# Expert stage of an attention-MoE kernel: nested blocks without else arms, one half block per expert behind the nest, and its branch announced in every block

## The chip, the cores and the metric

The kernel runs on one core of a Trainium2 chip. The metric is the device time of one execution in microseconds. A core has five engines with an instruction queue each: TensorE (PE), VectorE (DVE), ScalarE (ACT), GpSimd (POOL) and SyncE (SP). In the rows of the profile PE is shown as PE (matmuls) and PEld (weight loads); a name with q at its end (PEldq, ACTq, SPq) is what the sequencer of that engine does itself: jumps, register steps, semaphore steps.

## The reference

The work is attention inside chunks of 64 positions, a dense feed-forward layer, and a mixture of eight experts of which each token takes one:

```
attn = softmax over each chunk of 64 (q k^T / 8);  x = attn v, as 4608 tokens x 512
x    = relu(x @ w_in)^2 @ w_out                     # 512 -> 2048 -> 512
xn, en    = x and expert_emb, each row divided by its norm
expert    = argmax(xn @ en.T / tau);  gate = softmax(...)[expert]
for e in range(8):                                  # 512 -> 1024 -> 512
    out[tokens of e] = gate * (relu(x[tokens of e] @ w1[e]) @ w2[e])
```

How many tokens an expert has is known only on the chip. With the inputs of these runs experts 0 to 7 have 473, 448, 2029, 378, 256, 704, 192 and 128 tokens.

## The kernel before

The attention, the dense layer and the routing take the first 971 us and stand in straight code; the change touches of them only eight small operations behind the routing's last step (L499). The expert stage follows. Tokens of one expert are gathered from DRAM by their row numbers, 256 at a time (`TG`), turned by PE transposes (`turn`, L571), multiplied in three passes of a high and a low half with w1 (`first_product`, L594), passed through ReLU by ACT (L597) and DVE (L598), multiplied with w2 (`m2`, L413), scaled by the gate on ACT (L608) and scattered to the output by POOL (L609). Results of PE go through four PSUM banks in turn. 256 tokens are a full block; of the matmuls a full block has 96 of the first product, two second products of 24 and, between these, 8 transposes for the block that comes next. `short` (L960) is a half block of 128 tokens, with x as the stationary operand: 24 and 8 transposes (`sh`, `sht`) and 24, and with their weight loads some 116 instructions of PE.

The first block of an expert is straight code (`group`, L1020); in it, the weights of the next expert are loaded and split as well. For what is left, `more(e, g, ...)` (L990) is an `If` on the count: if more than 256 g + 128 tokens are there, a full block is computed and `more(e, g + 1)` stands inside it, 17 levels deep. Its else arm holds a second `If` (more than 256 g tokens?) around a half block. So the half block stands 17 times per expert in the program: first come the 17 full blocks in a row, then their else arms from the deepest one outwards, each ending with a semaphore step and a jump over the arms that follow. The way out of a nest at depth g is, on every engine: a jump to the else arm, taken because the count is too small; the second compare, which jumps over the half block or falls into it; a semaphore step that waits until what is queued on the engine is done; and, for g above 1, a jump over the other g - 1 arms to the next expert.

A jump can be announced: `mark_branch_hint_location` puts a register step and a hint instruction into each engine's queue that name the jump's place and whether it will be taken. Before, `more_e_(g+1)` is announced at the start of block g, and the jumps in and behind the else arm are not announced. Nothing reorders instructions around these places: each engine runs its queue in the order of the code, and PE's sequencer hands matmuls to a queue ahead of their execution, so that jumps are taken while earlier matmuls are still at work.

By the counts, experts 0 and 1 run two full blocks, expert 2 eight, expert 3 one and a half block, expert 4 one, expert 5 three, expert 6 one, and expert 7 only a half block. Expert 0's first block has run before 971 us.

## Time and profile before

| | us |
|---|---|
| median of three runs | 1430.68 (1430.56 to 1431.48) |
| the profiled execution, its own time | 1430.2 |
| its span in the profile | 1428.4 |
| PE busy in the span | 1367.7 (96%) |
| expert stage, from PE's first wait for its gathers to the end of the span | 971 to 1428.4 |

The busy share alone doesn't say where time could go: PE is close to full on average, and what idle time it has lies in few places. The view that lists PE's waits names what ended them; the timeline of PE gives their place; the instructions of the sequencer, grouped by line, give the length of each jump. A jump that the sequencer takes 4 us for is idle time of PE only as far as PE's queue runs empty behind it.

### The profile page before, as it was taken

To read this page: it belongs to the slowest core of one execution; us is meant where nothing else is said; L and a number is where in the kernel's file an instruction comes from. 1 tells how busy PE (TensorE), PEld (TensorE's weight loads), DVE (VectorE), ACT (ScalarE), POOL (GpSimd) and SP (SyncE) were. 2 spreads that over 40 slices of the span, in tenths; PEclk is the share of its full clock that TensorE was granted. 3 is DMA by queue.
4 is the path that set the end of the run, shared out by engine and by line. 5 is a ranking of instruction groups with operands and counts; after the bars stand their busy time and mean duration, and the time that the engine had idled before them with its cause. 6 is when DMAs were issued, how large, how long until landed. Compare 5 with 4: busy or idle time off the path is not lost. (4 is left out here: it accounts for less than half of the span.)

```text
span 1428.4 us, 27983 instructions
## 1 busy us (share of the span) xinstructions
PE 1367.7 (96%) x10780; PEld 1221.6 (86%) x10780; DVE 791.1 (55%) x2146; ACT 644.3 (45%) x1529; POOL 175.2 (12%) x189
## 2 busy tenths in 40 slices
PE   5699999999999999999999999998999999899998
PEld 4697889988998898899889988987889898788886
DVE  6878566657656675666576556754442222145424
ACT  4693535634553554355345535633442222145424
POOL 0000010000000100000100001323212121113110
PEclk6899999999999999999999999999999999999999
DMA  8533332122122212212212222136533111156412
GB/s 212 158 119 119 104 70 57 37 38 61 39 45 38 53 39 45 45 40 44 50 35 54 43 38 90 46 119 200 181 126 99 34 60 35 43 165 199 150 49 92
DMA packets 222794, 116.81 MB, mean 82 GB/s; under 512 B 191585, under 2 KB 192227, under 8 KB 222468
## 3 DMA queue, kind: packets, MB, share of 16 engines
q1 hardware_dynamic: 213508, 89.01, 23.9%
q0 software_dynamic: 9056, 25.35, 5.6%
q8 instruction: 99, 1.62, 0.5%
q14 instruction: 99, 0.81, 0.2%
q10 hardware_dynamic: 32, 0.02, 0.0%
HBM read 94.64 MB, written 20.19 MB: 80 GB/s over the span
## 5 line engine op out<-in xcount | busy, mean ns | idle before, releaser
L389 PE MATMUL l<-xT,wa 128*128 128x256 f32 x3168 | 382.6, 281 | 6.0 <-DVE wa L157 6.0
L389 PEld LDWEIGHTS l<-xT,wa 128*128 128x128 f32 x3168 | 378.1, 189 | 8.3 <-DVE wa L157 6.7
L413 PE MATMUL l<-wb,g 128*128 128x512 f32 x1536 | 373.2, 398 | 0.0
L413 PEld LDWEIGHTS l<-wb,g 128*128 128x128 f32 x1536 | 284.0, 188 | 65.7
L440 DVE CUSTOM_DVE_ANT_0 junk<-X,en 128x512 bf16<-128x512 f32 x240 | 166.3, 693 | 64.0 <-ACT X L433 60.8
L408 DVE TENSOR_TENSOR g<-l,g 128x256 fp32r<-128x256 f32 x264 | 110.3, 419 | 160.4 <-ACT g L405 157.1
L598 DVE SCALAR_TENSOR_TENSOR h<-m,h 128x256 fp32r<-128x256 f32 x144 | 60.9, 423 | 195.6 <-ACT h L597 189.0
L413 PE MATMUL m<-wa,h 128*128 128x512 f32 x576 | 139.3, 397 | 0.0
L399 ACT ACTIVATE l<-l 128x256 f32<-128x256 f32 x272 | 100.8, 371 | 68.6 <-PE l L389 60.7
L413 PEld LDWEIGHTS m<-wa,h 128*128 128x128 f32 x576 | 106.4, 188 | 24.2
L597 ACT ACTIVATE h<-m 128x256 fp32r<-128x256 f32 x144 | 55.1, 383 | 132.8 <-PE m L594 118.0
L405 ACT ACTIVATE g<-l 128x256 fp32r<-128x256 f32 x264 | 101.5, 384 | 8.5
L402 ACT ACTIVATE l<-l 128x256 f32<-128x256 f32 x272 | 100.1, 368 | 8.7
L490 POOL DMA_INDIRECT perm<-tid,pos x36 | 38.2, 1060 | 523.2 <-DVE pos L489 281.3
L594 PEld LDWEIGHTS m<-xc,wa 128*128 128x128 f32 x768 | 92.5, 189 | 0.6
L594 PE MATMUL m<-xc,wa 128*128 128x256 f32 x768 | 92.8, 281 | 0.0
L413 PE MATMUL m<-wb,h 128*128 128x512 f32 x336 | 81.9, 398 | 0.0
L609 POOL DMA_INDIRECT out_dram<-o,idx x38 | 38.5, 1014 | 326.9 <-ACT xc L79 140.1
L413 PEld LDWEIGHTS m<-wb,h 128*128 128x128 f32 x336 | 62.0, 188 | 14.1
L608 ACT ACTIVATE o<-m,gn 128x512 f32<-128x512 f32 x23 | 15.8, 688 | 114.6 <-PE m L413 71.2
L435 POOL TENSOR_TENSOR ss<-ss,half 128x1 f32<-128x1 f32 x36 | 28.1, 780 | 308.7 <-ACT l L434 165.2
L80 DVE TENSOR_TENSOR xc<-tp,xc 128x512 fp32r<-128x512 f32 x36 | 24.3, 684 | 69.1 <-ACT xc L79 69.1
(182 smaller groups left out, 1540.2 us busy)
## 6 DMA issues: line engine op xcount, KB each, us to landing
we<-in_moe_w_dram SPq DMA_DIRECT2D x124, 256.0 KB
v<-in_v_dram SPq DMA_DIRECT2D x144, 64.0 KB
x2d<-X SPq DMA_DIRECT2D x32, 258.0 KB
ws<-in_moe_w_in_dram SPq DMA_DIRECT2D x8, 1024.0 KB
ws<-in_moe_w_out_dram SPq DMA_DIRECT2D x8, 1024.0 KB
q<-in_q_dram SPq DMA_DIRECT2D x160, 32.0 KB
k<-in_k_dram SPq DMA_DIRECT2D x160, 32.0 KB
en<-embn SPq DMA_DIRECT2D x1, 2048.0 KB
```

The source lines that it names most:

```text
L389: PE.matmul(out=ps, lhsT=wi[:, a, m // 4, kt, (m % 4) * 128:(m % 4 + 1) * 128], rhs=x[b][:, :, kt, :], start=(n == 0), stop=(n == 3 * KD - 1),
L399: S.activation(out=ps, in_=ps, func=AF.Relu)
L402: S.activation(out=ps, in_=ps, func=AF.Square)
L405: S.activation(out=g[:, 0], in_=ps, func=AF.Copy)
L408: V.tensor_tensor(out=g[:, 1], in0=ps, in1=f32(g[:, 0]), op=ALU.subtract)
L413: PE.matmul(out=ps, lhsT=gs[kk][:, b, tt * 128:(tt + 1) * 128], rhs=wt[:, a, kk, :], start=(kk == 0 and n == 0), stop=(kk == last - 1 and ...
L440: V.tensor_tensor_reduce(out=junk.rearrange("p (g c) -> p g c", g=4), in0=rows(X)[:, :, 0:128], in1=en[:, e].rearrange("p (g c) -> p g c", ...
L490: G.indirect_dma_start(out=perm[:, :], out_offset=bass.IndirectOffsetOnAxis(ap=pos[:, 0:1], axis=0), in_=tid[:, i:i + 1], in_offset=None,)
L594: PE.matmul(out=ps, lhsT=v1[:, a, m // 4, kt, (m % 4) * 128:(m % 4 + 1) * 128], rhs=xt[:, b, :, kt, :], start=(n == 0), stop=(n == 3 * KD ...
L597: S.activation(out=g[:, 0], in_=ps, func=AF.Relu)
L598: V.scalar_tensor_tensor(out=g[:, 1], in0=ps, scalar=0.0, in1=f32(g[:, 0]), op0=ALU.max, op1=ALU.subtract)
L609: G.indirect_dma_start(out=out[:, :], out_offset=bass.IndirectOffsetOnAxis(ap=col, axis=0), in_=o, in_offset=None, bounds_check=NT - 1, oo ...
```

## The change

The else arms are gone. `more(e, g)` is an `If` with a full block and the next `more` in it, and nothing else. Behind the whole nest of an expert stands one `If`, `rest_e`, with the half block. Whether a half block is wanted is a second number per expert, computed on DVE behind the routing (L502 to L509 of the new code) and loaded with the counts, so that 16 numbers instead of 8 go into registers: `cnt[E + e]` is 256 for a count up to 256 and else (count - 1) modulo 256; below 128 the half block is run. The half block must find its gate values and row numbers in one place whatever the depth, so `tail` copies both (`gl`, `il`) at every turn, two operations of DVE of 128 x 1. `rest_e` is announced in every block, behind its first product; the announcement of the next `more` stays at the block's start. Expert 7 keeps an if with an else arm at its first branch.

The core of the diff:

```diff
-    ctf = per.tile([1, E], I32, name="ctf")
+    ctf = per.tile([1, 2 * E], I32, name="ctf")
...
-                V.tensor_copy(out=ctf, in_=carry[0:1, :])
+                V.tensor_copy(out=ctf[:, 0:E], in_=carry[0:1, :])
+                V.tensor_scalar_add(out=rem[:, 0:E], in0=carry[0:1, :], scalar1=-1.0)
+                V.tensor_copy(out=ctf[:, E:], in_=rem[:, 0:E])
...
+                V.tensor_copy(out=ctf[:, E:], in_=rem[:, E:2 * E])
...
-        def more(e, g, n, xt, ga):
-            with when(n > TG * g + 128, label=f"more_{e}_{g}", preferred_fallthrough_block=None if g else False) as full:
-                gan = gn[(g + 1) % 2]
+        def tail(e, g):
+            V.tensor_copy(out=gl, in_=gn[g % 2][:, 0:1])
+            V.tensor_copy(out=il, in_=idx[:, e, 2 * g:2 * g + 1])
+
+        def announce_rest(e):
+            tc.mark_branch_hint_location(f"rest_{e}", hint=cnt[E + e] < 128, engines=ENGS)
+
+        def block(e, g, xt, ga):
+            gan = gn[(g + 1) % 2]
+            Xn = gather(XN, cols(e, g + 1)) if g + 1 < MG else None
+            hs = first_product(e, xt)
+            announce_rest(e)
+            out2(e, g, hs, 0, ga)
+            if Xn:
+                turn(Xn, xc, gan)
+                tail(e, g + 1)
+            out2(e, g, hs, 1, ga)
+
+        def more(e, g):
+            with when(cnt[e] > TG * g + 128, label=f"more_{e}_{g}"):
                 if g + 1 < MG:
-                    tc.mark_branch_hint_location(f"more_{e}_{g + 1}", hint=n > TG * (g + 1) + 128, engines=ENGS)
-                Xn = gather(XN, cols(e, g + 1)) if g + 1 < MG else None
-                hs = first_product(e, xt)
-                out2(e, g, hs, 0, ga)
-                if Xn:
-                    turn(Xn, xc, gan)
-                out2(e, g, hs, 1, ga)
-                if Xn:
-                    more(e, g + 1, n, xc, gan)
-            with full.Else():
-                inner.append(full)
-                if e + 2 == E:
-                    tc.mark_branch_hint_location(f"more_{E - 1}_0", hint=cnt[E - 1] <= 128, engines=ENGS)
-                if g:
-                    with when(n > TG * g):
-                        short(e, g, xt, ga)
-                else:
-                    short(e, g, xt, ga)
-                inner.pop()
+                    tc.mark_branch_hint_location(f"more_{e}_{g + 1}", hint=cnt[e] > TG * (g + 1) + 128, engines=ENGS)
+                block(e, g, xc, gn[g % 2])
+                if g + 1 < MG:
+                    more(e, g + 1)
+
+        def rest(e):
+            more(e, 1)
+            with when(cnt[E + e] < 128, label=f"rest_{e}"):
+                short(e, il, xc, gl)
+
+        def announce(e):
+            tc.mark_branch_hint_location(f"more_{e}_1", hint=cnt[e] > TG + 128, engines=ENGS)
...
             hs = first_product(e, xt, each)
+            announce_rest(e)
             turn(second.pop(e), xc, gn[1])
+            tail(e, 1)
             out2(e, 0, hs, 0, ga, each)
             turn(Xe, xT, gx[(e + 1) % 2])
             out2(e, 0, hs, 1, ga)
-            more(e, 1, n, xc, gn[1])
+            rest(e)
```

In the order of the program the change shows on PE in two places. The first is a full block inside a nest, from the end of its first product (the row with `xc`) to the branch that leads into the next block; here the one before the deepest block of expert 2. `m` are PSUM banks, `wa` the expert's weights, `h` the first product's result, `tp` the transposes. Before:

```order
L594 MATMUL m_26731<-xc,wa 128x256 x12
L413 MATMUL m_26746<-wa,h 128x512 x24
L571 MATMUL tp<-ident,Xg 128x128 x8
L413 MATMUL m_26792<-wa,h 128x512 x24
L560 COMPARE_AND_BRANCH
L594 MATMUL m_26824<-xc,wa 128x256 x12
```

After:

```order
L604 MATMUL m_25037<-xc,wa 128x256 x12
L1005 REGISTER_ALU
L1104 BRANCH_PREFETCH_HINT
L416 MATMUL m_25067<-wa,h 128x512 x24
L581 MATMUL tp<-ident,Xg 128x128 x8
L416 MATMUL m_25115<-wa,h 128x512 x24
L570 COMPARE_AND_BRANCH
L604 MATMUL m_25147<-xc,wa 128x256 x12
```

Between the first product and the second one a register step and a hint have come in, which announce `rest_2`; branch, matmuls and transposes stand as they stood.

The second place is the end of expert 2's nest on PE: the second products of its deepest block, and what stands between them and the next expert (`sh` and `sht` are a half block's). Before, the start of the row of else arms:

```order
L413 MATMUL m_26951<-wa,h 128x512 x24
L413 MATMUL m_26981<-wa,h 128x512 x24
L560 UNCONDITIONAL_BRANCH
L560 COMPARE_AND_BRANCH
L971 MATMUL sh<-wa,xc 128x512 x18
L979 MATMUL sht<-ident,hr 128x128 x4
L971 MATMUL sh<-wa,xc 128x512 x6
L413 MATMUL m_27053<-wa,h 128x512 x3
L979 MATMUL sht<-ident,hr 128x128 x4
L413 MATMUL m_27053<-wa,h 128x512 x21
L560 UNCONDITIONAL_BRANCH x2
L560 COMPARE_AND_BRANCH
```

After:

```order
L416 MATMUL m_25289<-wa,h 128x512 x24
L416 MATMUL m_25319<-wa,h 128x512 x24
L570 UNCONDITIONAL_BRANCH x18
L570 COMPARE_AND_BRANCH
L981 MATMUL sh<-wa,xc 128x512 x18
L989 MATMUL sht<-ident,hr 128x128 x4
L981 MATMUL sh<-wa,xc 128x512 x6
L416 MATMUL m_25391<-wa,h 128x512 x3
L989 MATMUL sht<-ident,hr 128x128 x4
L416 MATMUL m_25391<-wa,h 128x512 x21
L570 UNCONDITIONAL_BRANCH x2
L1032 REGISTER_ALU
```

Before, the rows from the compare to the pair of jumps come again for each of the 17 depths. After, all depths have their semaphore step and jump side by side (the row x18), one compare and one half block follow, and then the next expert, whose first announcement is the last row shown.

## Rows read from the trace of the kernel before

**Rows 1.** The page: the span, and busy time of each engine

```profile
span 1428.4 us, 27983 instructions
...
PE 1367.7 (96%) x10780; PEld 1221.6 (86%) x10780; DVE 791.1 (55%) x2146; ACT 644.3 (45%) x1529; POOL 175.2 (12%) x189
```

**Rows 2.** PE's waits from 971 us on: releaser, us in total, times, longest

```profile
PE m L594 <- issue: 5.2, 1, 5.2
PE tp L571 <- DMA Xg<-x2d,idx: 3.2, 2, 2.1
```

**Rows 3.** PE's timeline: start us, us, group, [idle before <-releaser]

```profile
1004.18 11.54 PE L594 MATMUL m<-xT,wb 128*128 128x256 f32 x96 [1.04 <-ACT o L608]
...
1052.67 11.47 PE L594 MATMUL m<-xT,wa 128*128 128x256 f32 x96 [0.61 <-PEq L560]
...
1193.87 11.47 PE L594 MATMUL m<-xc,wa 128*128 128x256 f32 x96
...
1217.26 11.47 PE L594 MATMUL m<-xc,wa 128*128 128x256 f32 x96
...
1234.96 5.85 PE L413 MATMUL m<-wa,h 128*128 128x512 f32 x24
1246.06 13.49 PE L594 MATMUL m<-xT,wb 128*128 128x256 f32 x96 [5.25 <-issue]
...
1272.33 4.36 PE L971 MATMUL sh<-wb,xc 128*128 128x512 f32 x18
...
1311.51 13.01 PE L594 MATMUL m<-xT,wb 128*128 128x256 f32 x96 [2.59 <-PEq L560]
...
1385.10 11.54 PE L594 MATMUL m<-xT,wa 128*128 128x256 f32 x96 [0.85 <-ACT o L608]
...
1410.02 4.43 PE L971 MATMUL sh<-wb,xT 128*128 128x512 f32 x18 [0.43 <-PEq L560]
```

**Rows 4.** PE's jumps in seven windows: ns min/median/max, first and last start us

```profile
L560 PEldq COMPARE_BRANCH  x2: 393/2038/3684, 1236.5 to 1236.9; - x2
...
L560 PEldq EVENT_SEMAPHORE  x1: 51/51/51, 1240.9 to 1240.9; - x1
L560 PEldq COMPARE_BRANCH  x1: 4810/4810/4810, 1241.0 to 1241.0; - x1
...
L560 PEldq COMPARE_BRANCH  x1: 377/377/377, 1268.2 to 1268.2; - x1
...
L560 PEldq COMPARE_BRANCH  x2: 656/3206/5757, 1304.6 to 1305.3; - x2
...
L560 PEldq COMPARE_BRANCH  x1: 1588/1588/1588, 1405.3 to 1405.3; - x1
...
L560 PEldq COMPARE_BRANCH  x1: 3449/3449/3449, 1419.5 to 1419.5; - x1
...
L560 PEldq COMPARE_BRANCH  x6: 67/68/77, 1096.2 to 1213.1; - x6
```

**Rows 5.** Stretches of the expert stage: busy by engine, PEclk, DMA share, GB/s

```profile
1217.00:1234.00 17.00, 17.00 (x122) 15.86 (x121) 3.46 (x9) 3.75 (x9) 2.98 (x3) 1.00 0.15 47
1240.00:1260.00 20.00, 14.75 (x106) 14.28 (x105) 7.82 (x15) 7.43 (x17) 5.32 (x5) 0.83 0.45 136
1260.00:1280.00 20.00, 20.00 (x97) 16.14 (x96) 9.41 (x20) 10.02 (x20) 2.02 (x2) 1.00 0.57 174
1300.00:1320.00 20.00, 17.41 (x102) 15.50 (x101) 8.91 (x19) 8.01 (x16) 4.84 (x5) 0.91 0.53 173
```

**Rows 6.** Jumps of ACT's sequencer at the exit of expert 2

```profile
L560 ACTq COMPARE_BRANCH  x3: 38/56/64, 1240.9 to 1244.9; - x3
```

**Rows 7.** The lines of the small copies on DVE and of the counts' load

```profile
L573 DVE COPY gn<-Xg x24: 142/144/154, 971.1 to 1379.7; 128x1 f32<-128x1 f32 x24
...
L1037 SPq FUSED_REGOPS  x8: 13/147/187, 973.0 to 974.8; - x8
...
L1037 PEldq TENSOR_LOAD <-ctf x1: 783/783/783, 967.8 to 967.8; - x1
```

## Prediction

> **What bounds the kernel now.** I read the busy table of the page first: PE is busy for 1367.7 of 1428.4 us [rows 1], so the end moves only where PE's own work or its idle time moves. The change adds and removes no matmul on the path taken, so only idle time and clock are left. The second view is the list of PE's waits from 971 us, where the expert stage begins, to the end [rows 2]: 3.2 us are gathers at the stage's start, and nearly all of the rest stands at changes of expert, the largest being one wait of 5.2 us put down to "issue". The third view, PE's timeline, places them [rows 3]. Inside expert 2's nest of blocks there is no idle time: a block starts every 23.39 us (1193.87, 1217.26) and its first product takes 11.47. At the seven changes of expert PE stands still for 1.04 (0 to 1), 0.61 (1 to 2), 5.25 (2 to 3), nothing (after expert 3's half block), 2.59 (4 to 5), 0.85 (5 to 6) and 0.43 us (6 to 7); together 10.77. After the two long ones the first product is longer than 11.47 as well: 13.49 and 13.01, which is 2.02 and 1.54 more. [...] All that the exits of the nests cost is 10.77 + 2.02 + 1.54 = 14.33 us. This is the stake.

> The jumps of PE's sequencer say what an exit consists of [rows 4]. A jump that isn't taken inside the nest costs 0.07 us. A taken one that is announced and in time costs 0.38 to 0.39 (experts 3 and 2). The one in the else arm, not announced, cost 3.68 (expert 2) and 5.76 us (expert 4), the unannounced jump over the other arms 4.81 (expert 2). Two announced ones were late all the same, 0.66 and 1.59 us (experts 4 and 6). Not every one of these microseconds reaches PE: at expert 2 the first jump begins at 1236.5, and the matmuls already queued last until 1240.81 (the second product starts at 1234.96 and takes 5.85). So 4.3 us of an exit are covered, and the 3.68 of the second jump lies wholly under them. Then comes the small semaphore step (0.05 us) that waits until the queue has drained, at 1240.9, and whatever a jump costs behind that is bare: the 4.81 is nearly all of the 5.25.

> **The change part by part.** *Removed: the else arms.* Before, an exit from depth g takes the announced jump into its else arm, an unannounced second jump over the half block, the drain step, and for g above 1 an unannounced jump over g-1 arms. After, it takes the announced jump to a short row of drain steps, one drain step with a near jump, and then the jump `rest_e` over the one half block, followed by a second drain step. If every announcement does its work, the exits of experts 2 and 4 lose their bare 4.81 and what stands bare of the 5.76, with the clock loss behind them.

> *Added: one jump and one drain step at the bare end.* An announced jump in time is 0.4 us, a drain step 0.05. Before, the bare end of an exit showed 0.43 to 1.04 us where nothing was late; I take 0.3 to 0.5 more for each.

> *Added: the second announcement.* Each block now carries two: `more_e_(g+1)` at its start and `rest_e` behind the first product. In before there is never a second one before the branch of the first, so no row shows what the sequencer does with two. The bounds: both are kept (nothing lost), or the second takes the place of the first (the first jump then costs what unannounced jumps cost, 3.45 to 5.76 us). The nearest rows are the late announced ones, 1.59 us for expert 6 though it was announced at the start of that expert, about 20 us earlier: so an announcement by itself doesn't bring the code; it has to be the valid one when the sequencer comes near the jump. That reads like one place that is looked up late, not like a list of fetches under way, and I take the second bound as the likelier.

> *What a late first jump does.* Alone it is covered: 3.68 against 4.3. But behind it stands `rest_e`, and its target can hardly be fetched earlier than the code that holds the jump. Two fetches in a row are 3.68 + 3.45 = 7.13 us (3.45: the unannounced jump at the program's end [rows 4]); less the cover of 4.3 that leaves 2.8 bare, and with the restart of PE, 0.6 to 1.0 where nothing is late, 3.5 us. A gap of 2.59 cost 1.54 of clock and one of 5.25 cost 2.02, so 1.7 for this one: 5.2 us at an exit where the first jump comes late.

> *How many exits.* Between none and all six (0, 1, 2, 4, 5, 6) I take half, with experts 2, 5 and 6 as the ones, since the order shows the last announcement of `more` a whole block, some 300 PE instructions, ahead of its branch, and some of these will have been acted on before the second comes. [...]

> *Expert 3.* Its exit falls into the half block instead of over it. Transfers are dense there (DMA share 0.57 against 0.15 in a steady block [rows 5]), and the late jump of expert 4 under 0.53 took 5.76. If its first jump is late as well, 5.76 from 1268.2 [rows 4] end at 1274.0, where the half block before starts at 1272.33 with no gap: 1.6 bare, 0.7 of restart, 1.5 of clock, 3.8.

> *Other engines.* ACT and DVE have the same jumps; ACT's three in the exit of expert 2 stretch from 1240.9 to 1244.9 [rows 6]. PE needs neither for its first four banks of the next product, 5.6 us at 1.4 us each (11.47 / 8), so up to there they cost nothing; two late ones in a row on ACT would come close, and I take 0. The two small copies a turn are 0.14 us each on DVE [rows 7], which is 55% busy. The seven small operations behind the counts (1.0 us), the longer load of 16 counts (0.78 on PE now) and SP's eight more register steps (0.147 each, 1.2 us [rows 7]) lie before the gathers that PE waits for, or beside them: 0, and 1.5 if the cover is gone. The announcements are two register steps a block on each queue, in the shadow of queued work.

> *The sum.* Experts 0, 1, 4: 1.25 + 1.0 + 1.0 (the gaps of before plus a jump, and expert 4 without its late one). Experts 2, 5, 6: 3 x 5.2 = 15.6. Expert 3: 3.8. Together 22.65 against 14.33 before: +8.3. On the profiled execution's own 1430.2 us that is 1438.5; the median of the runs stands 0.5 above that execution, so I say **1439 us**.

> **The rivals.** *A, the other side: both announcements hold.* Its place is the sequencer of PE in the last block of each expert, its price one jump in time (0.4 us) more an exit and no late one. The changes of expert then cost 1.3, 1.0, 1.1, 0.5, 0.9, 1.1 and 0.9 = 6.8 us, 7.5 less than before: 1422.7, or 1423 beside the median. It decides if no more than one exit is late, since one (4.1) still leaves a gain of 3.4 and two leave none. For it: announced jumps at 0.38 and 0.39 do what they should, and the code on the way is shorter and nearer. Against it: the announced 0.66 and 1.59.

> *B. As much is lost as won.* The second announcement displaces the first at two places only, so that what experts 2 and 4 win (7.27 - 1.1 and 4.13 - 0.9, together 9.4) goes to expert 3 (3.8), one other (5.2 - 0.9 = 4.3) and the added jumps (1.3): 1430, between 1427.5 and 1433.

> *D. All six exits are late*, because no jump that stands behind two announcements is in time: three more exits at 5.2 instead of about 1.1 add 12.3, so 1451. The late jumps of 3.45 to 5.76 speak for it, the 0.38 and 0.39 against it. [...]

> *C. The change doesn't do what it says,* because other engines set PE's start (ACT behind two late jumps of its own): 1 to 3 us on top of A or B, inside their ranges.

> **How the numbers follow.** My forecast, S, with two to four late exits, 0.55; D 0.05; A 0.27; B 0.13. The likeliest gives 1439; its own range is 1433 to 1447, the upper end with up to 2 us more each in experts 1 and 4, where an announced target could be fetched in place of the code that comes next. The range of 8 in 10 runs from 1422, which takes in most of A, to 1444, and leaves out D and the upper part of S. About 0.2% (2.9 us) is what a measurement can tell from no change: faster than that 0.27, within it 0.13, slower 0.60.

> **What would show it.** The timeline at the changes of expert: right, if PE's gaps before experts 3, 6 and 7 are about 3.5 us each with a first product longer than 11.47, with gaps at 1 and 2 near 1; PE's first jumps there last 3 us or more, and the `rest` jump behind them again as long. Rival A shows all jumps at 0.4 and no gap above 1.4. The forecast is wrong in its step on the second announcement if the first jumps stay at 0.4; wrong in the cover if they are late and PE doesn't stop; wrong on the other engines if PE's waits name ACT or DVE with more than 1 us at an exit. Inside expert 2's nest the blocks should still start every 23.39 us.

## The result, and the profile after

The changed kernel takes 1446.1 us (median of four runs, 1443.6 to 1450.4) where the kernel before took 1430.7 beside it (median of three; a fourth run of it, 3433.4 us, is left out and isn't explained): a ratio of 1.0104, with a 95% interval of 1.0088 to 1.0119. It is slower, as forecast, but by 15 us where 8 were forecast, and outside the range. The profiled execution is the slowest of the four, 1450.4 us, 20.2 above that of before; the rows below are of that one.

The page of the changed kernel, span and busy time, against [rows 1]:

```profile
span 1448.7 us, 28256 instructions
...
PE 1380.2 (95%) x10780; PEld 1232.7 (85%) x10780; DVE 794.4 (55%) x2189; ACT 644.4 (44%) x1529; POOL 174.2 (12%) x189
```

PE has as many matmuls as before, but they are busy for 12.5 us more (1380.2 against 1367.7), and the span grew by 20.3. The expert stage by itself (length, then busy time of PE, PEld, DVE, ACT and POOL, granted clock, DMA share, GB/s), before:

```profile
971.00:1429.00 458.00, 436.78 (x2765) 390.30 (x2763) 158.03 (x344) 159.44 (x335) 89.46 (x90) 0.98 0.34 108
```

and after:

```profile
971.00:1449.00 478.00, 445.39 (x2766) 397.89 (x2764) 161.38 (x382) 159.15 (x336) 88.36 (x89) 0.96 0.33 104
```

3.8 of the 12.5 us lie ahead of 971 us (934.77 against 930.96) and cost nothing: the stage begins where it began (its first transposes start at 972.09 against 971.95). In the stage PE is busy for 8.6 us more, at a lower granted clock, and idle for nearly 12 more. So somewhat less than half of the loss is matmuls at a lower clock, and the rest is idle time. The list of PE's waits from 971 us on says what stands ahead of it (releaser, us in total, times, longest; against [rows 2]):

```profile
PE m L604 <- PEq L570: 10.5, 4, 4.4
PE sh L981 <- ACTq L570: 6.1, 2, 3.1
PE m L604 <- issue: 4.7, 2, 2.7
PE tp L581 <- DMA Xg<-x2d,idx: 3.8, 2, 2.8
```

21.3 us are waits for sequencers (PE's own, ACT's, and "issue"), against 8.9 before (5.25, 2.59, 0.61 and 0.43 in [rows 3]). The gathers cost about what they did (3.8 us against 3.2). PE's timeline shows the places (start, us, group, idle time before and its releaser; against [rows 3]):

```profile
1007.00 14.11 PE L604 MATMUL m<-xT,wb 128*128 128x256 f32 x96 [3.72 <-PEq L570]
...
1058.38 11.47 PE L604 MATMUL m<-xT,wa 128*128 128x256 f32 x96 [1.05 <-ACT o L618]
...
1198.95 11.37 PE L604 MATMUL m<-xc,wa 128*128 128x256 f32 x96
...
1222.21 11.37 PE L604 MATMUL m<-xc,wa 128*128 128x256 f32 x96
...
1246.76 1.08 PE L604 MATMUL m<-xT,wb 128*128 128x256 f32 x7 [1.13 <-PEq L570]
1250.54 12.66 PE L604 MATMUL m<-xT,wb 128*128 128x256 f32 x89 [2.70 <-issue]
...
1279.23 5.95 PE L981 MATMUL sh<-wb,xc 128*128 128x512 f32 x18 [3.10 <-ACTq L570]
...
1322.15 13.69 PE L604 MATMUL m<-xT,wb 128*128 128x256 f32 x96 [4.39 <-PEq L570]
...
1396.60 1.43 PE L604 MATMUL m<-xT,wa 128*128 128x256 f32 x10 [1.25 <-PEq L570]
1400.01 12.63 PE L604 MATMUL m<-xT,wa 128*128 128x256 f32 x86 [1.98 <-issue]
...
1428.59 5.99 PE L981 MATMUL sh<-wb,xT 128*128 128x512 f32 x18 [3.00 <-ACTq L570]
```

Blocks in the nest start every 23.26 us (1198.95, 1222.21) and their first product takes 11.37. Against that, change of expert by change of expert:

| into expert | gap before | clock before | gap after | clock after |
|---|---|---|---|---|
| 1 | 1.04 | 0 | 3.72 | 2.74 |
| 2 | 0.61 | 0 | 1.05 | 0.1 |
| 3 | 5.25 | 2.02 | 1.13 + 2.70 | 2.37 |
| half block of 3 | 0 | 0 | 3.10 | 1.59 |
| 5 | 2.59 | 1.54 | 4.39 | 2.32 |
| 6 | 0.85 | 0 | 1.25 + 1.98 | 2.69 |
| 7 | 0.43 | 0 | 3.00 | 1.56 |
| sum | 10.8 | 3.6 | 22.3 | 13.4 |

(The clock column is the time of the first product above 11.37 after and 11.47 before, of the half block's first group above 4.36 to 4.43.) That is 35.7 us against 14.3, 21.4 more. The 11.47 that the prediction used is the time inside a nest; the first block of an expert is straight code, and expert 4's, behind no gap, takes 11.36 before and 11.37 after, so the clock column of before is some 0.5 too low in all. The 10 blocks inside the nests of experts 1, 2 and 5 are 0.13 us shorter each, which gives back 1.3. With both taken off, 19.6 of the 20.3 are accounted for.

The stretches behind the gaps, busy by engine, granted clock and share of the transfers, against [rows 5]:

```profile
1000.00:1020.00 20.00, 16.28 (x103) 15.32 (x102) 6.71 (x12) 6.36 (x14) 5.38 (x5) 0.83 0.42 128
1246.00:1264.00 18.00, 14.54 (x105) 14.46 (x106) 7.98 (x15) 7.39 (x17) 4.88 (x5) 0.81 0.51 155
...
1318.00:1338.00 20.00, 15.85 (x111) 15.59 (x112) 9.07 (x18) 8.87 (x20) 4.87 (x5) 0.83 0.51 157
```

The granted clock is 0.81 to 0.83 behind three of the gaps, where a steady block had 1.00. Within these stretches it was 0.50 from 1006.1 to 1012.8, from 1248.5 to 1255.2 and from 1320.1 to 1326.8 us, and 1.00 right behind. And PE's first jump at each exit, in the order of the experts 0 to 6 (ns min/median/max, first and last start, against [rows 4]):

```profile
L570 PEldq COMPARE_BRANCH  x1: 4296/4296/4296, 998.9 to 998.9; - x1
...
L570 PEldq COMPARE_BRANCH  x1: 245/245/245, 1053.0 to 1053.0; - x1
...
L570 PEldq COMPARE_BRANCH  x1: 3642/3642/3642, 1241.3 to 1241.3; - x1
...
L570 PEldq COMPARE_BRANCH  x1: 5080/5080/5080, 1271.8 to 1271.8; - x1
...
L570 PEldq COMPARE_BRANCH  x1: 7892/7892/7892, 1313.4 to 1313.4; - x1
...
L570 PEldq COMPARE_BRANCH  x1: 3488/3488/3488, 1391.0 to 1391.0; - x1
...
L570 PEldq COMPARE_BRANCH  x1: 3655/3655/3655, 1421.2 to 1421.2; - x1
```

Six of seven are late, 3.5 to 7.9 us, that of expert 1 alone is in time. Into each of the six falls one packet of the queue q8, whose kind is instruction (104 packets and 1.70 MB on the page), into that of expert 1 none. Before, the same jumps took 0.37 to 0.66 at experts 0 to 5 and 1.59 at 6. Their announcements are still in the program, where they were; new behind them are those of the half blocks and, at expert 6, that of expert 7's branch, which stood in an else arm before.

### The profile page after: what moved, and what is told of

The parts are those of the page before. It is cut to its first block, busy times and chain, and to the rows that moved or that the text cites. A ratio compares the mean times of both kernels' runs of the same rounds, so it can differ in the third digit from the quotient of the medians.

```text
span 1448.7 us, 28256 instructions
## 1 busy us (share of the span) xinstructions
PE 1380.2 (95%) x10780; PEld 1232.7 (85%) x10780; DVE 794.4 (55%) x2189; ACT 644.4 (44%) x1529; POOL 174.2 (12%) x189
```

## The experiments

**1. Which announcement is in force.** The theory of the prediction: the later of two announcements takes the place of the earlier. The rival: both are kept, and the new order of the code makes the first jumps late. Four kernels. The first, `only_more`, leaves out the new announcement:

```diff
         def block(e, g, xt, ga):
...
             hs = first_product(e, xt)
-            announce_rest(e)
...
-        tc.mark_branch_hint_location("rest_0", hint=cnt[E] < 128, engines=ENGS)
```

> Only the announcement of the next block's branch is left; the half block's branch isn't announced at all. Theory 1 (a second announcement takes the place of the first): the first jumps of PE's sequencer at the exits of experts 0 to 5 are back at 0.2 to 0.7 us (they were 3.5 to 7.9), that of expert 6 stays late (3 to 4 us), because the branch of expert 7 is announced right behind it; the unannounced jump over the half block costs little, since its target lies within the code that is read on anyway; 1424 to 1430 us. Theory 2 (both announcements are kept, and the new order of the code makes the first jumps late): first jumps stay at 3.5 us and more, 1440 us or above. Theory 3 (theory 1, but the unannounced jump over the half block is late and bare): first jumps in time, the jump behind the drain step 3 to 5 us at every exit, 1440 to 1450 us.

It took 1433.6 us, 1.0011 of before (0.9996 to 1.0025), so 13 us of the loss go with this one announcement. The first jumps of experts 0, 1, 3 and 5 are back at 0.37 to 0.41 us. Expert 6's stays late (3.69, and 2.77 for the jump behind it), as expected, since the announcement for expert 7 follows its own at once. Experts 2 and 4 are a miss: 4.24 and 3.11 us though announced alone, covered by the queue (gaps of 1.07 and 0.80). So at these two a late jump needs no second announcement. In `swap` below they are in time, but there the branch is also announced later, behind the first product; a kernel with this one announcement at that place was not run, so for 2 and 4 the place of the announcement is a rival. The jump over the half block, announced nowhere, takes 0.24 to 0.45 us at experts 0, 1, 2 and 5, so theory 3 falls: it needed no announcement there. That code is read on without a jump, the changed kernel's trace shows: 53 packets of q8 come between 100 and 900 us, ahead of the first jump of any engine (977.8). That the target lies in such code is an estimate: between 1096 and 1213.5 us, in expert 2's nest, q8 brings 6 packets, one in 19.6 us, while PE runs a block of some 300 instructions in 23.26, so a packet of PE's code would reach further than the 116 instructions to the target. Which packets are PE's, the trace doesn't tell.

`swap` keeps both and exchanges their places:

```diff
             hs = first_product(e, xt)
-            announce_rest(e)
+            if g + 1 < MG:
+                announce(e, g + 1)
...
-                if g + 1 < MG:
-                    tc.mark_branch_hint_location(f"more_{e}_{g + 1}", hint=cnt[e] > TG * (g + 1) + 128, engines=ENGS)
+                announce_rest(e)
                 block(e, g, xc, gn[g % 2])
...
-            announce(e)
+            announce_rest(e)
...
             hs = first_product(e, xt, each)
-            announce_rest(e)
+            announce(e)
```

> Both announcements are in every block as in the changed kernel, but the half block's branch is announced at the block's start and the next block's branch behind the first product. Theory 1 (the later one takes the place of the earlier): first jumps at 0.2 to 0.7 us at all seven exits, expert 6 too, 1422 to 1428 us. Theory 2 (both are kept, or the number of announcements costs by itself): as the changed kernel, first jumps 3.5 us and more, 1443 to 1450 us. Theory 3: first jumps in time, the jump over the half block 3 to 5 us and bare, 1440 to 1450 us.

1430.1 us, 0.9989 of before (0.9979 to 0.9998): 16 us less than the changed kernel, by the order of two announcements. PE's first jumps at the exits of experts 2, 3, 4 and 6 in the trace of `swap`:

```profile
L570 PEldq COMPARE_BRANCH  x1: 373/373/373, 1237.9 to 1237.9; - x1
...
L570 PEldq COMPARE_BRANCH  x1: 363/363/363, 1263.9 to 1263.9; - x1
...
L570 PEldq COMPARE_BRANCH  x1: 378/378/378, 1306.0 to 1306.0; - x1
...
L570 PEldq COMPARE_BRANCH  x1: 383/383/383, 1403.6 to 1403.6; - x1
```

All seven are at 0.36 to 0.39. With as many announcements in the same blocks, the number of them is no cause. The time is 2 us above what was expected, and the timeline of `swap` tells where that stands:

```profile
1006.20 11.55 PE L604 MATMUL m<-xT,wb 128*128 128x256 f32 x96 [1.41 <-PEq L570]
...
1055.01 11.46 PE L604 MATMUL m<-xT,wa 128*128 128x256 f32 x96 [1.04 <-ACT o L618]
...
1243.42 11.57 PE L604 MATMUL m<-xT,wb 128*128 128x256 f32 x96 [1.16 <-PEq L570]
...
1271.78 6.00 PE L981 MATMUL sh<-wb,xc 128*128 128x512 f32 x18 [3.55 <-ACTq L570]
...
1311.18 11.58 PE L604 MATMUL m<-xT,wb 128*128 128x256 f32 x96 [0.86 <-ACT o L618]
...
1383.45 11.57 PE L604 MATMUL m<-xT,wa 128*128 128x256 f32 x96 [1.23 <-ACT o L618]
...
1409.02 4.44 PE L981 MATMUL sh<-wb,xT 128*128 128x512 f32 x18 [1.07 <-ACT o L618]
```

Every gap is near 1 us, as rival A of the prediction had it, but for one: before the half block of expert 3 PE waits 3.55 us, which ACT's sequencer ends, and its first group then takes 6.00 us, where it took 4.36 in the kernel before. That is experiment 2.

`only_rest` takes the other announcement away, that of the next block's branch:

```diff
-                if g + 1 < MG:
-                    tc.mark_branch_hint_location(f"more_{e}_{g + 1}", hint=cnt[e] > TG * (g + 1) + 128, engines=ENGS)
                 block(e, g, xc, gn[g % 2])
...
             each = lambda: e_split(w_p, "w")
-            announce(e)
```

> Only the announcement of the half block's branch is left. Theory 1: the announcements of the next block's branch did nothing in the changed kernel except at expert 1, so this one stands where the changed kernel stands, or up to 5 us above it: 1443 to 1452 us, first jumps 3.5 to 8 us at all seven exits. Theory 2 (both were kept): the first jumps lose an announcement that worked, and the time goes up by 4 us or more for several exits, above 1455 us.

1451.6 us, 1.0146 of before (1.0123 to 1.0168), 5 above the changed kernel. All seven first jumps are late, 3.67 to 7.24 us. So in the changed kernel the announcement of the next block's branch was worth one exit, that of expert 1, which is what its trace shows.

`before_two` puts a second, true announcement into the blocks of the kernel before:

```diff
+        def announce_far(e):
+            if e + 2 < E:
+                tc.mark_branch_hint_location(f"more_{e + 1}_1", hint=cnt[e + 1] > TG + 128, engines=ENGS)
...
                 hs = first_product(e, xt)
+                announce_far(e)
                 out2(e, g, hs, 0, ga)
...
             hs = first_product(e, xt, each)
+            announce_far(e)
```

> The kernel before with its else arms, and one more announcement in every block of experts 0 to 5, behind the first product: that of the first branch of the next expert's nest, a true one, but too early. Theory 1: it takes the place of the announcement made at the block's start, so the first jumps of experts 0 to 5 become late (3.5 us and more instead of 0.4 to 0.7), the second jumps begin later and stand bare: 1438 to 1455 us. Theory 2 (both are kept): first jumps stay at 0.4 to 0.7 us, 1430 to 1433 us.

1438.8 us, 1.0053 of before (1.0036 to 1.0069). The old code, with its else arms, becomes slower by an announcement that is only added. PE's first jumps at experts 0, 1, 2 and 3:

```profile
L560 PEldq COMPARE_BRANCH  x1: 382/382/382, 1001.3 to 1001.3; - x1
...
L560 PEldq COMPARE_BRANCH  x1: 3634/3634/3634, 1050.8 to 1050.8; - x1
...
L560 PEldq COMPARE_BRANCH  x1: 370/370/370, 1243.5 to 1243.5; - x1
...
L560 PEldq COMPARE_BRANCH  x1: 6135/6135/6135, 1274.6 to 1274.6; - x1
```

Two became late, 3.63 and 6.14 us (experts 1 and 3); those of 0, 2, 4 and 5 stayed at 0.37 to 0.38. Theory 1 had named all six, so its form is too strong: the first announcement isn't lost in every block. A reading that fits is that it is lost only where it hasn't been acted on when the second one comes; no run shows that moment. The added instructions also move code, and other jumps changed with them (expert 4's second one fell from 5.76 to 0.22 us, expert 6's first from 1.59 to 0.36), so at a single exit this kernel can't part the announcement from the place. `swap`, with as many announcements as the changed kernel, is the cleaner test.

**2. What stops PE at the half block of expert 3.** In the changed kernel the jumps of ACT around that place, with the line of who waited for them:

```profile
L570 ACTq COMPARE_BRANCH  x2: 51/54/57, 1276.2 to 1279.2; - x2
L570 ACTq EVENT_SEMAPHORE  x1: 17/17/17, 1279.2 to 1279.2; - x1
...
  PE sh L981: 3.1, 1
```

ACT's first jump starts at 1276.2, the semaphore step behind it only at 1279.2, and PE's half block at 1279.23. Before, PE went into the half block with no gap [rows 3]. Theory 4: behind the nest the half block's operand `xc` and its banks count as written inside the nest, so PE has to wait until ACT has jumped out of it; in an else arm at the first depth it doesn't. `swap_else` puts the half block back there, for that depth alone:

```diff
         def rest(e):
-            more(e, 1)
-            with when(cnt[E + e] < 128, label=f"rest_{e}"):
-                short(e, il, xc, gl)
...
+            with when(cnt[e] > TG + 128, label=f"more_{e}_1") as full:
+                announce_rest(e)
+                block(e, 1, xc, gn[1])
+                more(e, 2)
+                with when(cnt[E + e] < 128, label=f"rest_{e}"):
+                    short(e, il, xc, gl)
+            with full.Else():
+                inner.append(full)
+                with when(cnt[e] > TG):
+                    short(e, idx[:, e, 2:3], xc, gn[1][:, 0:1])
+                inner.pop()
```

> The swapped announcements, and for the first depth of a nest the half block again in an else arm of its own; for all deeper exits the one half block behind the nest stays. Theory 4 (PE's half block of expert 3 waits 3.0 to 3.6 us because, behind the nest, its operands and banks count as written in the nest, so that PE must wait until ACT has made its own late jump out of it): in the else arm the wait is gone as in the kernel before, PE goes on into the half block with a gap of at most 0.5 us and at the full clock, 5 us less than the swapped kernel: 1423 to 1427 us. Rival 5 (ACT's late jump stops PE in either place): gap of 3 us stays, 1429 to 1431 us.

1421.2 us, 0.9921 of before (0.9906 to 0.9937): below the expected 1423, and 11 us better than before. In its timeline the gaps that were expensive are these (into expert 3, its half block, into expert 5):

```profile
1241.32 11.48 PE L604 MATMUL m<-xT,wb 128*128 128x256 f32 x96 [1.33 <-PEq L570]
...
1265.59 4.37 PE L981 MATMUL sh<-wb,xc 128*128 128x512 f32 x18
...
1302.35 11.55 PE L604 MATMUL m<-xT,wb 128*128 128x256 f32 x96 [0.15 <-PEq L570]
```

No gap before the half block and no lost clock; the seven gaps add up to 5.7 us (1.20, 1.09, 1.33, 0, 0.15, 1.51, 0.43) where they were 10.8 before. With 3.6 of clock and 1.3 of shorter blocks in the nests that makes 10.0 of the 10.1 us between the two profiled spans (1428.4 and 1418.3). So the wait goes with the place of the half block; whether it is the operand or the banks that tie it to ACT's jump, no run parts. A second set of runs gave 1421.1 us, 0.9935 (0.9919 to 0.9952):

> The swapped announcements with the else arm at the first depth once more, beside the three that follow: 1419 to 1423 us, 0.7 to 0.9% below the kernel before.

**3. Whether ACT's announcements do anything.** In the changed kernel ACT took 3.0 us from its first jump at expert 3 to the semaphore step behind it (1276.2 to 1279.2), although its jumps were announced. `swap_pe` announces on PE's queue alone (`ENGS = [ET.PE]`):

> The swapped kernel with announcements on PE's queue alone; ACT, DVE, POOL and SP get none. Theory 6 (on ACT the code of many blocks fits into one piece of code that was entered long before the announcement, so the announcement comes too late to be acted on and its jumps wait 2.4 to 3.4 us announced or not): ACT's time between its first jump at an exit and the step behind it stays at 2.4 to 3.6 us, and the time stays at 1428 to 1432 us. Rival 7 (ACT's announcements do shorten its jumps): that time grows to 4 us or more, PE waits for ACT at more exits, 1435 us or above.

ACT's jumps at the exit of expert 3 in `swap`, with all announcements:

```profile
L570 ACTq COMPARE_BRANCH  x2: 40/50/59, 1268.3 to 1271.8; - x2
L570 ACTq EVENT_SEMAPHORE  x1: 17/17/17, 1271.7 to 1271.7; - x1
```

and in `swap_pe`, with none on ACT:

```profile
L570 ACTq COMPARE_BRANCH  x2: 40/42/45, 1268.6 to 1271.4; - x2
L570 ACTq EVENT_SEMAPHORE  x1: 17/17/17, 1271.3 to 1271.3; - x1
```

From the first jump to the semaphore step ACT takes 3.4 us with announcements and 2.7 without; at the other exits it is 2.4 to 2.8 in both kernels. So they buy nothing on ACT; why not (that ACT has entered the code long before they come) was argued and not tested. The time, 1426.0 us or 0.9956 of before (0.9941 to 0.9971), is 2 us below what was expected and lower than that of `swap`, which ran on another chip; its profiled run, 1429.7, is the slowest of its four. Side by side with the better kernel there is no difference (1421.2 with announcements on PE alone, 0.9942, against 1421.1), so what lowered `swap_pe` stays open:

> The same with announcements on PE's queue alone. If those on ACT, DVE, POOL and SP do nothing here (theory 6): the same time as beside it, within 2 us. If they cost (each is two register steps a block on those queues, and the swapped kernel without them stood at 0.9956 of before against 0.9989 with them): 3 to 5 us less, 1416 to 1418 us.

**4. Whether the place of the code decides.** In the changed kernel PE stops twice in the middle of a first product, after 7 matmuls (2.70 us) and after 10 (1.98), with no semaphore to wait for. `after_shift` moves all of PE's code by 4 instructions:

```diff
-        for _ in range(40):
+        for _ in range(42):
             PE.matmul(out=warm[:, 0, 0:128], lhsT=ones, rhs=ones, start=True, stop=True)
```

> The changed kernel with two more warm-up matmuls of PE at its very start, so that all code of PE behind them is moved by 4 instructions (a matmul and its weight load each). Theory 8 (the stops of 2.70 and 1.98 us inside the first products of experts 3 and 6, 7 and 10 matmuls after their start, are PE's sequencer waiting for the next piece of code, at a fixed place in the program): the stops come 2 matmuls earlier, after 5 and 8. Rival 9 (they wait for something in time, another engine or the length of the jump): they stay at 7 and 10, or move irregularly. Time 1443 to 1452 us.

Neither theory has it right. The stops are gone, not moved. In their stead the jump over the half block became late at the same two exits (2.64 and 2.85 us instead of 0.24), so it looks as if the same wait now stood at the jump and not 7 or 10 matmuls behind it; that it is the same one was not tested. PE's first jumps of experts 0, 2 and 4 in its trace:

```profile
L570 PEldq COMPARE_BRANCH  x1: 407/407/407, 1000.6 to 1000.6; - x1
...
L570 PEldq COMPARE_BRANCH  x1: 4350/4350/4350, 1238.1 to 1238.1; - x1
...
L570 PEldq COMPARE_BRANCH  x1: 248/248/248, 1307.2 to 1307.2; - x1
```

Experts 0 and 4 are in time, where they took 4.30 and 7.89 us in the changed kernel; late are now 2, 3, 5 and 6. The one run took 1440.6 us, below all four of the changed kernel. As far as one run can tell, four instructions decide on two exits and some 5 us; by what means was not shown.

Do the other kernels hang on the place as well? `before_shift` and `swap_else_shift` have the same edit:

> The kernel before with all of PE's code moved by 4 instructions. If the late unannounced jumps of experts 2 (4.81 us behind the drain) and 4 (5.76 us) belong to the order of the code: within 2 us of before. If they hang on where the code lies: other exits are late, and the time moves by 3 us or more either way.

1429.8 us, 0.9998 of before (0.9988 to 1.0009); the late jumps are the ones of before (3.68 and 4.80 at expert 2, 5.68 at 4, 1.76 at 6).

> The same as the first of these, with all of PE's code moved by 4 instructions (two more warm-up matmuls at the start). If the gain comes from the announcement that is in force last, and not from where the code happens to lie: first jumps stay at 0.2 to 0.7 us and the time within 2 us. If it is the place: one or more exits become late, 3 to 6 us each.

1421.0 us, 0.9936 (0.9920 to 0.9953), first jumps at 0.36 to 0.46. So neither hangs on it by that much, and the changed kernel does. That this is because in it one announcement races the other is argued; `swap` itself was not moved.

## Why the prediction was wrong

**The bound** was right. The loss stands where 14.3 us stood before, at the changes of expert, in gaps and clock; the blocks inside the nest still have no idle time. They start every 23.26 us, not the 23.39 that was foretold.

**The second announcement** was right in its direction: of two, the later one counted in these runs and the earlier was mostly lost. `only_more` shows it at experts 0, 3 and 5, whose jumps are in time again without the second one (0.37 to 0.41 us), `swap` at 6 (0.38 against 3.66 us), and `only_rest` and `before_two` agree; rival A, that both hold, is out. At 2 and 4 the second announcement isn't shown to be the whole cause (4.24 and 3.11 us in `only_more`). Why the earlier one holds at some exits (expert 1 in the changed kernel, 0.25 us; 0 and 4 too once the code is moved, 0.41 and 0.25) stays open. That an announcement has to be the valid one when the sequencer comes near the jump was the author's reading of one late jump (1.59 us); no run shows that moment.

**The number of exits** is the term that failed. The prediction put half of the six as late (2, 5 and 6) and expert 3 besides; measured were all but expert 1. Experts 0 and 4 were priced at 1.25 and 1.0 us and cost 6.5 and 6.7: 10.9 of the 13 us by which the sum of 22.65 fell short of 35.7. The set that was named, 2, 3, 5 and 6, is the set of `after_shift`, four instructions away, and that its 1440.6 us lie beside the forecast of 1439 is luck: nothing in the prediction fixes the place to four instructions. No run shows why the late ones should be 2, 5 and 6, on which the 15.6 us of the sum rest: that was the author's estimate, and the runs showed 0, 2, 3, 4, 5 and 6 late in the changed kernel and 2, 3, 5 and 6 four instructions further on. What failed was to fix the late exits by it, and to leave the case of nearly all exits late (rival D, 1451) at 0.05 and out of the range; the 1446.1 us lie 2 above its upper end.

**The price of a late exit**, 5.2 us, was near: 6.2 at expert 2, 5.9 at 5, 4.6 at 6. Its parts were not as told. The second jump was expected late behind the first; in the profiled run it is so only at experts 0 and 6 (2.75 and 2.31), while at 2 and 5 it took 0.24 and the wait came 7 and 10 matmuls into the product. At expert 4 the first jump alone (7.89) outlasted the cover. And the clock took more than the 1.7 assumed: 2.3 to 2.7 at the full blocks. The late first jumps took 3.5 to 4.3 us at a DMA share of 0.20 to 0.23 (experts 0, 2, 5, 6), 5.1 and 7.9 at 0.76 and 0.60 (experts 3 and 4).

**Expert 3** was priced at 3.8 and cost 4.7, and came near for the wrong reason, which is luck: it is not PE's late jump that decides there but ACT's. In `swap` PE's jump is in time (0.36 us), and the gap is 3.55 all the same. So the step "other engines", which took ACT at 0 since PE has four banks of cover, failed too, by the prediction's own sign of more than 1 us put down to ACT. At the full blocks of `swap` no wait for ACT is above 1.23; the half block behind the nest waits for ACT's jump itself. Experiment 2 prices it: `swap_else` stands 9 us below `swap`, which ran on another chip, and 4.9 below `swap_pe`, which ran beside it; the gap with its clock is 5.2 (3.55 and 1.6). Of the rest of the 9, 2.3 lie ahead of the first change of expert, where the trace of `swap_else` is that much earlier (1003.87 against 1006.20), and aren't explained by the edit.

**The small operations** at 0: the transposes that open the stage start 0.14 us later than before, so they cost nothing that shows.

## What to carry to other kernels

Announce one branch at a time, and rather the jump out of a nest than the one over a half block. With a second announcement behind the first, six of seven first jumps took 3.5 to 7.9 us here, and with the two exchanged all seven took 0.36 to 0.39. The jump over the half block, some 116 instructions, took 0.24 to 0.45 us without any announcement at four exits of `only_more`, and 2.77 behind a late one. Before moving a shared tail behind a conditional nest, look at who then has to wait for the jump out of it on the other engines: in `swap` PE waited 3.55 us for ACT before expert 3's half block, and in `swap_else`, with a copy in an else arm, not at all. When an argument turns on where code happens to lie, give the bad case for all places its share of the range.

## What the runs showed of the hardware that was not expected

```profile
1278.99 4.47 PE L981 MATMUL sh<-wb,xc 128*128 128x512 f32 x18 [3.10 <-ACTq L570]
...
1398.67 11.56 PE L604 MATMUL m<-xT,wa 128*128 128x256 f32 x96 [3.35 <-ACTq L570]
```

Behind no gap the half block's first group took 4.36 in the kernel before, and a first product 11.37 in the changed one. The changed kernel's gap of 3.10 before the same half block cost 1.59, at a granted clock of 0.50 from 1279.2 to 1282.4. And a block in the nest takes 23.26 us in the changed kernel and all made from it, 23.39 in the kernel before and in `before_two`, with most of the difference in the first product (11.37 against 11.47); the cause was not looked for.
